# Converting float64 weights in the tile that keeps them, and two tiles instead of four in the head of a fused attention and MLP kernel

## The chip, the cores and the metric

The kernel runs on one core of one Trainium2 chip. The metric is the device time of one execution in microseconds (us). The engines are named as in the profile: PE (TensorE, with PEld for its weight loads), DVE (VectorE), ACT (ScalarE), POOL (GpSimd) and SP (SyncE), which issues nearly all DMA transfers. Each engine works off its own list of instructions strictly in order.

## The reference, cut to what matters

Three layers follow each other: an attention (a downsampled one plus a local band), a softplus MLP, and an expert layer that picks one expert for each token. Only the first two and the weights of the second bear on the change:

```python
x = attn_out.transpose(0, 2, 1, 3).reshape(B * S, H * D)   # 2304 tokens x 512
h = x @ w_in                                                # 512 x 2048
g = np.maximum(h, 0.0) + np.log1p(np.exp(-np.abs(h)))       # softplus
x = g @ w_out                                               # 2048 x 512
...                                                         # top-1 expert layer
```

`w_in` and `w_out` arrive as float64 (each is a float32 array times a float64 scalar). The engines work in float32, so the kernel has to convert both, 2 x 1 M values, on the chip.

## The kernel before

**Tiles of weights.** The hidden width of 2048 is cut into 16 chunks of 128. Chunk c has one tile of `w_in` (called i0 to i15 here, kept in `wi[:, c]`) and one of `w_out` (o0 to o15, kept in `wo[:, c]`), each 128 x 512. The list `conv` sets the order of conversion: i0, i1, o0, i2, o1, i3, o2, i4, o3 and so on to o15, 32 tiles.

**Conversion of one tile.** `load_raw` issues a DMA of 512 KB into one of six buffers named `raw`, in which every value is two 32-bit words. The same six buffers hold the raw q, k and v of the attention for batches 1 to 3 (`qr`, `kr`, `vr`), so loads of both kinds wait for each other's buffers. Then one instruction on ACT, `f64_top` (L617, called the *top* below), reads the upper words and writes 32 bits that hold the exponent and the high mantissa bits. Three instructions on DVE in `from_f64` finish the tile: a shift (L625), a merge of the sign (L628) and a merge of the low mantissa bits (L629). The last of them writes the tile of `wi` or `wo`; with it the raw buffer is free. Between the top and L629 the value lives in a tile `cva`, of which there are two, so that a top waits until the L629 of the tile before the last is done:

```python
t = mlp.tile([128, 512], I32, tag="cva", name="cva", bufs=2)
A.activation(t.bitcast(F32), raw[:, :, 1].bitcast(F32), AF.Abs, scale=F64_REBIAS)
```

**Head.** The first 18 steps (`HEAD`) run the attention of batch 0, software-pipelined in stages. `conv_to(n)` is called from step 4 on and converts up to tile n of the list; until the head ends its instructions are given priority over the rest (`ahead(-50)`). With the counts of this kernel the head converts four tiles: i0, i1, o0, i2.

**Block 0.** The MLP goes in six blocks of 384 tokens. Block 0 uses plain float32 matmuls (`xN` with `wi`, L768; for the first eight chunks `gN` with `wo`, L809). For chunk c the PE makes `ph`, ACT makes the softplus's Abs, Exp and Ln (L777, L778, L779), DVE adds the positive part and writes `gN` (L786), and the PE multiplies `gN` with `wo[:, c]` into `py`. The remaining tiles are converted during block 0, two for each chunk, and the attention of batch 1 runs between (its results `pS`, `pA`, `pO`). Blocks 1 to 5 and the expert layer need no more conversions.

**What sets the order.** The order on each engine isn't written out: a scheduler places the instructions by priority, program order and its own estimate of times when the program is built. A change in tiles or in the place of a call can therefore move neighbours as well.

Of the kernel before, what the change touches and what calls it, by code (L numbers as in the profile page):

```python
# [9 lines left out]
F32 = mybir.dt.float32  # L10
F32R = mybir.dt.float32r
I32 = mybir.dt.int32
U32 = mybir.dt.uint32
AF = mybir.ActivationFunctionType
ALU = mybir.AluOpType
# [26 lines left out]
F64_REBIAS = 2.0 ** -112  # L42
# [6 lines left out]
LAG = LAGS[-1]  # L49
HEAD = 12 + LAG  # L50
C0 = 3
CR = 1

NATIVE = 1


@with_exitstack
def band_attention__softplus_mlp__top1_moe(
# [15 lines left out]
    V, A, G, T = nc.vector, nc.scalar, nc.gpsimd, nc.tensor  # L74
# [28 lines left out]
    mlp = ctx.enter_context(tc.tile_pool(name="mlp", bufs=2))  # L103
    wi = wpool.tile([128, NC1, CC, 128], F32, name="wi")
    wo = wpool.tile([128, NC1, DM], F32, name="wo")
    ydram = drp.tile([NB, 128, CC, TB], F32, name="ydram")

    def ahead(n):

        return tc.high_priority(n) if n else nullcontext()  # L110
# [187 lines left out]
    class Local:  # L298
# [58 lines left out]
        def st_PV(self):  # L357
# [7 lines left out]
            if blk not in xT:  # L365
                if blk < NATIVE:
                    xT[blk] = xpool.tile([128, CC, TB], F32, tag="xT", name="xN")
                else:
                    xT[blk] = xpool.tile([128, 2, CC, TB], F32R, tag="xT", name="xT")
            if blk < NATIVE:  # L370
                xf = xT[blk][:, self.hp, off:off + TH].rearrange("p (g r) -> p g r", r=FACTOR)
            else:
# [5 lines left out]
                in1=odb.to_broadcast([128, TH // FACTOR, FACTOR]), op=ALU.add)  # L378
            if blk < NATIVE:
                return  # L380
# [201 lines left out]
    def attn_to(p):  # L582
        while pos[0] < p:
            _, n, st = pieces[pos[0]]
            pos[0] += 1
            run_piece(n, st)

    done = set(x[1:] for x in pieces)
    for n in range(NOLD):
        for st in range(6):  # L590
            if (n, st) not in done:
                late = n >= 14
                t = {3: 8.0, 4: 8.6 if late else 8.0, 5: 9.0 if late else 8.3}[st]
# [18 lines left out]
                    )  # L612


    def f64_top(raw):
        t = mlp.tile([128, 512], I32, tag="cva", name="cva", bufs=2)
        A.activation(t.bitcast(F32), raw[:, :, 1].bitcast(F32), AF.Abs, scale=F64_REBIAS)  # L617
        return t

    def from_f64(raw, t, dst):  # L620

        lo, hi = raw[:, :, 0], raw[:, :, 1]
        ins = V.tensor_scalar(t, t, 3, None, ALU.logical_shift_left)  # L625
        if started[0]:
            tc.keep_in_program_order(ins)
        V.scalar_tensor_tensor(t, hi, -0x80000000, t, ALU.bitwise_and, ALU.bitwise_or)  # L628
        V.scalar_tensor_tensor(dst.bitcast(I32), lo, 29, t, ALU.logical_shift_right, ALU.bitwise_or)  # L629

    conv = [("i", 0), ("i", 1), ("o", 0)]
    for c in range(1, NC1):
        conv += ([("i", c + 1)] if c + 1 < NC1 else []) + [("o", c)]
    cpos, lpos = [0], [0]
    raws, tops = {}, {}

    def load_raw(n):
        while lpos[0] < min(n, len(conv)):
            kind, c = conv[lpos[0]]
            raw = mlp.tile([128, 512, 2], I32, tag="raw", name="raw", bufs=RAWB)  # L640
            if kind == "i":
                nc.sync.dma_start(
                    out=raw.rearrange("p (c f) w -> p c (f w)", c=CC),
                    in_=w_in[:, c * 128:(c + 1) * 128].bitcast(I32).rearrange("(c p) f -> p c f", p=128))
            else:
                nc.sync.dma_start(out=raw.rearrange("p f w -> p (f w)"),
                                  in_=w_out[c * 128:(c + 1) * 128, :].bitcast(I32))
            raws[lpos[0]] = raw
            lpos[0] += 1

    def conv_to(n):
        while cpos[0] < min(n, len(conv)):
            i = cpos[0]
            load_raw(i + 2)
            kind, c = conv[i]
            with ahead(0 if started[0] else -50):
                for k in range(i, min(i + 2, lpos[0]) if started[0] else i + 1):
                    if k not in tops:
                        tops[k] = f64_top(raws[k])
                from_f64(raws.pop(i), tops.pop(i), wi[:, c].rearrange("p c f -> p (c f)") if kind == "i" else wo[:, c, :])  # L660
            cpos[0] += 1
            load_raw(i + 2)

# [9 lines left out]
    def split_wi(n, c):  # L673
        if n < NATIVE:
            return
        wis[n, c] = split(wi[:, c] if n < NB else mo["w1"][:, :, c * 128:(c + 1) * 128], "wis")

    def plain_g(n, c):

        return n < NATIVE and c < NC1 // 2  # L680

# [80 lines left out]
    def mlp_H(n, c):  # L762
        ps = psa.tile([128, 512], F32, tag="pa", name="ph")
        wt = None if n < NATIVE else wis.pop((n, c))
        i = 0
# [257 lines left out]
    for st in range(HEAD):  # L1023
        attn_to(pre_end[st])
        if st >= C0 - 5 + LAG:
            conv_to((st - C0 + 5 - LAG) * CR // 4 + 1)
        if st == 9 + LAG:
            split_wi(0, 0)
    started[0] = True
# [15 lines left out]
    for i, (n, c) in enumerate(seq[:NMLP]):  # L1045
# [20 lines left out]
        if n == 0:  # L1066
            conv_to(max(cpos[0], 3 + 2 * c + 1, CB + (33 - CB) * (2 * c + 1) // 32))
# [21 lines left out]
        if n == 0:  # L1089
            conv_to(max(cpos[0], 3 + 2 * c + 2, CB + (33 - CB) * (2 * c + 2) // 32))  # L1090
# [97 lines left out]
    p, q, pos_q = stages[-1]  # L1188
# [57 lines left out]
```

## Time and profile before

| | |
|---|---|
| time, median of 3 runs | 764.23 us (763.49 to 765.17) |
| time of the profiled execution | 765.59 us |
| its span, first to last instruction | 763.8 us |
| PE busy | 734.5 us, 96% of the span |
| DVE, ACT, POOL busy | 487.6, 462.3, 419.2 us |

The profiled execution took 1.8 us more than its span and 1.36 us more than the median. Times in the rows further down count from the start of the span. "Busy" means that an instruction is in the engine; for PE this includes matmuls that run slowly or overlap, so a busy PE isn't a PE at its peak.

### The profile page before, as it was taken

What the parts mean: (1) busy time and instruction counts of PE and PEld (TensorE: products, weight loads), DVE (VectorE), ACT (ScalarE), POOL (GpSimd) and SP (SyncE); (2) the same over time, 40 slices, a digit from 0 to 9 for tenths busy, and PEclk for the clock granted to TensorE, in tenths of its full rate; (3) what the DMA queues carried; (4) which work ended last, traced back from release to release, by engine and by line L of the source; (5) the groups of instructions that cost most, each with busy time, mean ns of one, the idle gap of its engine ahead of it and who ended that gap; (6) DMA issues with size and microseconds to landing.
All of it is one profiled execution on the core that took longest, in us unless ns stands there. A gap on an engine that the chain in (4) does not pass through costs nothing.

```text
span 763.8 us, 13608 instructions
## 1 busy us (share of the span) xinstructions
PE 734.5 (96%) x4917; PEld 655.8 (86%) x4918; DVE 487.6 (64%) x933; ACT 462.3 (61%) x1196; POOL 419.2 (55%) x381
## 2 busy tenths in 40 slices
PE   5989899999999999999999999999999999999995
PEld 5765567699999999998999999999997989899894
DVE  6999779765879555788645554346994484284222
ACT  5955565676667757666766665666864364365332
POOL 3553207376565655665565656666778465455542
PEclk9989999999999999999999999999999999999999
DMA  8987755115230511241001100530011022002002
GB/s 190 203 188 195 226 165 177 45 39 106 50 75 9 112 33 23 42 87 42 14 2 23 43 1 1 221 125 1 4 68 55 21 63 83 0 1 83 1 0 88
DMA packets 111446, 55.45 MB, mean 73 GB/s; under 512 B 89593, under 2 KB 102411, under 8 KB 111371
## 3 DMA queue, kind: packets, MB, share of 16 engines
q1 hardware_dynamic: 111083, 53.98, 26.8%
q8 instruction: 41, 0.67, 0.4%
q10 hardware_dynamic: 288, 0.52, 0.2%
q14 instruction: 34, 0.28, 0.1%
HBM read 45.05 MB, written 9.44 MB: 71 GB/s over the span
## 4 chain that ended last, share of the span: by engine, by line
PE 69%; DVE 16%; ACT 4%; issue 4%; DMA 3%; POOL 2%; SPq 1%; DVEq 0%; ACTq 0%; POOLq 0%
PE ph L771 19%; PE py L812 19%; PE py L1130 11%; PE ph L973 9%; PE pS L462 2%; DVE cva L628 2%; PE pO L495 2%; DVE cva L625 2%; PE pA L488 1%; PE py L809 1%; DVE xs L954 1%; DMA vr<-in_v_dram 1%; DVE wi L629 1%; DMA raw<-in_moe_w_in_dram 1%; PE ph L768 1%
## 5 line engine op out<-in xcount | busy, mean ns | idle before, releaser
L812 PE MATMUL py<-g,wos 128*128 128x384 f32 x1056 | 209.1, 341 | 2.6 <-DVE y L818 1.2
L812 PEld LDWEIGHTS py<-g,wos 128*128 128x128 f32 x1056 | 182.6, 188 | 9.2 <-issue 1.4
L771 PE MATMUL ph<-xT,wis 128*128 128x384 f32 x960 | 182.2, 337 | 0.0
L771 PEld LDWEIGHTS ph<-xT,wis 128*128 128x128 f32 x960 | 166.7, 188 | 1.1
L668 POOL TENSOR_TENSOR wis<-wi,wis 128x512 fp32r<-128x512 f32 x80 | 104.1, 1304 | 73.0 <-ACT wis L667 66.2
L668 POOL TENSOR_TENSOR wos<-wo,wos 128x512 fp32r<-128x512 f32 x88 | 118.2, 1344 | 45.0 <-ACT wos L667 44.7
L777 ACT ACTIVATE ga<-ph 128x384 f32<-128x384 f32 x96 | 46.6, 485 | 64.3 <-PE ph L771 61.3
L793 DVE SCALAR_TENSOR_TENSOR ph<-ph,ga 128x384 f32<-128x384 f32 x80 | 44.7, 560 | 58.9 <-ACT ga L779 58.6
L973 PE MATMUL ph<-xs,ws 128*128 128x384 f32 x378 | 73.9, 336 | 1.2 <-DVE u L978 1.2
L978 DVE TENSOR_TENSOR u<-ph,u 128x384 f32<-128x384 f32 x60 | 33.3, 555 | 60.2 <-PE ph L973 59.9
L973 PEld LDWEIGHTS ph<-xs,ws 128*128 128x128 f32 x378 | 67.1, 188 | 4.8 <-DVE u L978 1.6
L667 ACT CAST wos<-wo 128x512 fp32r<-128x512 f32 x88 | 54.4, 618 | 26.4 <-PE py L812 23.6
L1130 PE MATMUL py<-wos,gs 128*128 128x512 f32 x270 | 69.0, 394 | 0.7 <-POOL gs L984 0.4
L1130 PEld LDWEIGHTS py<-wos,gs 128*128 128x128 f32 x270 | 50.0, 188 | 9.8 <-POOL gs L984 0.8
L668 POOL TENSOR_TENSOR wos<-w2s,wos 128x512 fp32r<-128x512 f32 x24 | 33.5, 1395 | 34.7 <-ACT wos L667 34.7
L779 ACT ACTIVATE ga<-ga 128x384 f32<-128x384 f32 x96 | 50.3, 525 | 2.1
L778 ACT ACTIVATE ga<-ga 128x384 f32<-128x384 f32 x96 | 50.3, 525 | 0.3
L481 POOL TENSOR_TENSOR pls<-pls,plst 128x420 f32<-128x420 f32 x18 | 16.0, 891 | 61.2 <-DVE plst L480 54.4
L475 ACT ACTIVATE pls<-pls,plst 128x70 f32<-128x70 f32 x108 | 36.7, 341 | 21.4 <-DVE plst L473 21.3
L794 DVE CAST g<-ph 128x384 fp32r<-128x384 f32 x80 | 44.0, 550 | 7.8 <-PE py L812 4.3
L667 ACT CAST wis<-wi 128x512 fp32r<-128x512 f32 x80 | 48.9, 611 | 0.0
L768 PE MATMUL ph<-xN,wi 128*128 128x384 f32 x128 | 45.6, 503 | 0.9 <-DVE gN L786 0.9
(195 smaller groups left out, 1232.4 us busy)
## 6 DMA issues: line engine op xcount, KB each, us to landing
raw<-in_moe_w_in_dram SPq DMA_DIRECT2D x16, 512.0 KB
raw<-in_moe_w_out_dram SPq DMA_DIRECT2D x16, 512.0 KB
lv<-in_v_dram SPq DMA_DIRECT2D x72, 70.0 KB
vr<-in_v_dram SPq DMA_DIRECT2D x16, 288.0 KB
ydram<-y SPq DMA_DIRECT2D x12, 384.0 KB
yb<-ydram SPq DMA_DIRECT2D x12, 384.0 KB
out_dram<-ob SPq DMA_DIRECT2D x16, 256.0 KB
qr<-in_q_dram SPq DMA_DIRECT2D x48, 72.0 KB
```

What stands on the lines that cost most here:

```text
L667: A.copy(w[:, 0], src)
L668: G.tensor_tensor(out=w[:, 1], in0=src, in1=w[:, 0].bitcast(F32), op=ALU.subtract)
L768: T.matmul(ps[:, :TB], wi[:, c, cc, :], xT[n][:, cc, :], start=(cc == 0), stop=(cc == CC - 1))
L771: T.matmul(ps[:, :TB], wt[:, w, cc, :], xT[n][:, x, cc, :], start=(i == 0), stop=(i == 3 * CC - 1))
L777: A.activation(a, ps[:, :TB], AF.Abs)
L778: A.activation(a, a, AF.Exp, scale=-1.0)
L779: A.activation(a, a, AF.Ln, bias=1.0)
L793: V.scalar_tensor_tensor(o, ps[:, :TB], 0.0, a, ALU.max, ALU.add)
L794: (A.copy if n < NATIVE else V.tensor_copy)(g[:, 0, :], o)
L812: T.matmul(yps[n][dc][:, :TB], w[:, a, dsl], g[:, b, :], start=(c == 0 and i == 0), stop=(c == NC1 - 1 and i == 2))
L973: T.matmul(ps[:, :TB], ops[:, w, a, cc, :], xop[p, x][:, l, cc, :], start=i == 0, stop=i == 5)
L1130: T.matmul(yps[n][t], g[:, a, t * 128:(t + 1) * 128], w[:, b, :], start=first and c == q and i == 0, stop=last and c == q + NQ and i == 2)
```

## The change

The tile `cva` goes. The top writes its 32 bits straight into the place in `wi` or `wo` where the weights will stand, and the three DVE instructions work there in place. And the head's `conv_to` is capped at `HEADC = 2`: it converts i0 and i1; o0 and i2 are converted when block 0's first call of `conv_to` asks for them.

```diff
+HEADC = 2
...
-    def f64_top(raw):
-        t = mlp.tile([128, 512], I32, tag="cva", name="cva", bufs=2)
-        A.activation(t.bitcast(F32), raw[:, :, 1].bitcast(F32), AF.Abs, scale=F64_REBIAS)
-        return t
+    def f64_top(raw, dst):
+        A.activation(dst, raw[:, :, 1].bitcast(F32), AF.Abs, scale=F64_REBIAS)
...
-    def from_f64(raw, t, dst):
+    def from_f64(raw, dst):
...
-        lo, hi = raw[:, :, 0], raw[:, :, 1]
+        lo, hi, t = raw[:, :, 0], raw[:, :, 1], dst.bitcast(I32)
         ins = V.tensor_scalar(t, t, 3, None, ALU.logical_shift_left)
...
         V.scalar_tensor_tensor(t, hi, -0x80000000, t, ALU.bitwise_and, ALU.bitwise_or)
-        V.scalar_tensor_tensor(dst.bitcast(I32), lo, 29, t, ALU.logical_shift_right, ALU.bitwise_or)
+        V.scalar_tensor_tensor(t, lo, 29, t, ALU.logical_shift_right, ALU.bitwise_or)
...
+    def weights(i):
+        kind, c = conv[i]
+        return wi[:, c].rearrange("p c f -> p (c f)") if kind == "i" else wo[:, c, :]
...
-                    if k not in tops:
-                        tops[k] = f64_top(raws[k])
-                from_f64(raws.pop(i), tops.pop(i), wi[:, c].rearrange("p c f -> p (c f)") if kind == "i" else wo[:, c, :])
+                    if k not in topped:
+                        topped.add(k)
+                        f64_top(raws[k], weights(k))
+                from_f64(raws.pop(i), weights(i))
...
-            conv_to((st - C0 + 5 - LAG) * CR // 4 + 1)
+            conv_to(min((st - C0 + 5 - LAG) * CR // 4 + 1, HEADC))
```

The lines of the changed kernel shift by one up to L617, where the top keeps its number; its DVE instructions are L624, L627 and L628, the softplus L781 to L783, `gN` L790. The scheduler then places things anew. Three places matter below.

**DVE at the end of the head.** `xN` (L376, then L377) is the last piece of block 0's input; the transposes of `qr` and `kr` belong to batch 1. Before:

```order
L335 TENSOR_REDUCE lst<-ls 128x3
L180 STREAM_TRANSPOSE qkT<-qr 128x576
L333 SCALAR_TENSOR_TENSOR ls<-pS,mask 128x210
L355 COPY laT<-pA 70x384
L204 TENSOR_REDUCE dqs<-qkT 128x144
L376 TENSOR_TENSOR xN<-pO,od 128x192
```

and now, where the `wi` rows are the conversion of i2:

```order
L627 SCALAR_TENSOR_TENSOR wi<-raw,wi 128x512
L347 RECIPROCAL lst<-lst 128x3
L336 TENSOR_REDUCE lst<-ls 128x3
L334 SCALAR_TENSOR_TENSOR ls<-pS,mask 128x210
L356 COPY laT<-pA 70x384
L181 STREAM_TRANSPOSE qkT<-qr 128x576
L628 SCALAR_TENSOR_TENSOR wi<-raw,wi 128x512
L377 TENSOR_TENSOR xN<-pO,od 128x192
```

Three of the four instructions from the transpose to `xN` moved away (ahead of the transpose or behind `xN`), and the last step of i2 came in. The conversion of o0 stands some 15 rows earlier; before, o0 and i2 were converted in the middle of the head.

**ACT at the first softplus of block 0.** `ga_887` (now `ga_871`) is chunk 0's softplus, `xT` a cast for block 1. Before:

```order
L341 ACTIVATE ls_845,lst_847<-ls_845,lst_847 128x70 x3
L384 CAST xT_918<-xf_919 128x192
L777 ACTIVATE ga_887<-ph_882 128x384
L778 ACTIVATE ga_887<-ga_887 128x384
L384 CAST xT_918<-xf_930 128x192
L779 ACTIVATE ga_887<-ga_887 128x384
```

and now, with the tops of i4 (`raw_957`) and o3 (`raw_984`):

```order
L342 ACTIVATE ls_836,lst_838<-ls_836,lst_838 128x70 x3
L617 ACTIVATE wi_95<-raw_957 128x512
L385 CAST xT_912<-xf_913 128x192
L781 ACTIVATE ga_871<-ph_866 128x384
L617 ACTIVATE wo_96<-raw_984 128x512
L782 ACTIVATE ga_871<-ga_871 128x384
L385 CAST xT_912<-xf_924 128x192
L783 ACTIVATE ga_871<-ga_871 128x384
```

Two tops stand among the first softplus's instructions. The load of i4 takes the raw buffer that i2's L628 frees; before, it took the one that the transpose of `qr` frees.

**ACT at chunk 3's softplus.** Before (`raw_1101` is i6, `raw_1120` is o5):

```order
L416 ACTIVATE pde_1050,pdn_1049<-pS_1040,pmx_1048 96x144 x3
L617 ACTIVATE cva_1103<-raw_1101 128x512
L777 ACTIVATE ga_1076<-ph_1071 128x384
L778 ACTIVATE ga_1076<-ga_1076 128x384
L617 ACTIVATE cva_1122<-raw_1120 128x512
L779 ACTIVATE ga_1076<-ga_1076 128x384
```

and now (`raw_1108`, `raw_1120`, `raw_1135` and `raw_1147` are o5, i7, o6 and i8):

```order
L417 ACTIVATE pde_1040,pdn_1039<-pS_1030,pmx_1038 96x144 x3
L617 ACTIVATE wo_96<-raw_1108 128x512
L617 ACTIVATE wi_95<-raw_1120 128x512
L617 ACTIVATE wo_96<-raw_1135 128x512
L781 ACTIVATE ga_1066<-ph_1061 128x384
L782 ACTIVATE ga_1066<-ga_1066 128x384
L617 ACTIVATE wi_95<-raw_1147 128x512
L783 ACTIVATE ga_1066<-ga_1066 128x384
```

The tops run three tiles further ahead here than before, and one still stands between Exp and Ln. On DVE, the conversion of i6 and the first step of i8 stand ahead of chunk 3's `gN` (before, that of i6 alone).

## Rows read from the trace of the kernel before

**Rows 1.** The page: PE's busy time, and the chain that ended last by engine.

```profile
PE 734.5 (96%) x4917; PEld 655.8 (86%) x4918; DVE 487.6 (64%) x933; ACT 462.3 (61%) x1196; POOL 419.2 (55%) x381
...
PE 69%; DVE 16%; ACT 4%; issue 4%; DMA 3%; POOL 2%; SPq 1%; DVEq 0%; ACTq 0%; POOLq 0%
```

**Rows 2.** Windows by stage; columns as its first line says.

```profile
core 0: us, PE busy (x) PEld busy (x) DVE busy (x) ACT busy (x) POOL busy (x), PEclk, DMA share, GB/s
0.00:55.00 55.00, 42.95 (x434) 35.23 (x436) 45.23 (x105) 37.07 (x137) 26.30 (x54) 0.96 0.89 196
55.00:162.00 107.00, 102.00 (x566) 69.17 (x563) 86.14 (x149) 65.10 (x181) 38.14 (x37) 0.97 0.52 147
162.00:764.00 602.00, 589.52 (x3923) 551.42 (x3922) 356.19 (x682) 360.17 (x881) 354.76 (x291) 1.00 0.17 48
```

**Rows 3.** Waits: who waited for whom, us in total, times, longest.

```profile
ACT cva L617 <- DVE wi L629: 12.7, 8, 2.3
...
ACT cva L617 <- DVE wo L629: 11.0, 10, 2.3
```

**Rows 4.** DVE groups of 33.9 to 43.2 us: count, busy us, mean ns, idle before.

```profile
L628 DVE SCALAR_TENSOR_TENSOR cva<-raw,cva 128x512 int32<-128x512 int32 x2 | 2.5, 1270 | 0.0
L625 DVE TENSOR_SCALAR cva<-cva 128x512 int32<-128x512 int32 x2 | 0.8, 417 | 0.0
L629 DVE SCALAR_TENSOR_TENSOR wi<-raw,cva 128x512 int32<-128x512 int32 x1 | 0.7, 693 | 0.0
L629 DVE SCALAR_TENSOR_TENSOR wo<-raw,cva 128x512 int32<-128x512 int32 x1 | 0.7, 673 | 0.0
```

**Rows 5.** Conversion instructions by line: ns min/median/max, first and last start.

```profile
L625 DVE TENSOR_SCALAR cva<-cva x32: 376/416/2464, 28.7 to 154.6; 128x512 int32<-128x512 int32 x32
...
L628 DVE SCALAR_TENSOR_TENSOR cva<-raw,cva x32: 650/691/1652, 29.6 to 155.5; 128x512 int32<-128x512 int32 x32
```

**Rows 6.** Timeline, end of the head: start us, us, instruction, [idle before <- releaser].

```profile
50.41 0.68 ACT L617 ACTIVATE cva<-raw 128x512 f32<-128x512 f32 x1 [0.31 <-DMA raw<-in_moe_w_in_dram]
...
54.78 0.78 DVE L180 STREAM_TRANSPOSE qkT<-qr 128x576 f32<-128x576 f32 x1 [0.33 <-DMA qr<-in_q_dram]
...
55.69 0.39 SPq L642 DMA_DIRECT2D raw<-in_moe_w_in_dram  x1
...
56.87 0.34 DVE L376 TENSOR_TENSOR xN<-pO,od 128x192 f32<-128x192 f32 x1
...
60.48 0.49 ACT L777 ACTIVATE ga<-ph 128x384 f32<-128x384 f32 x1
```

**Rows 7.** Timeline around chunk 3's softplus, 82 to 88.5 us.

```profile
82.01 0.69 DVE L629 SCALAR_TENSOR_TENSOR wi<-raw,cva 128x512 int32<-128x512 int32 x1
...
82.77 0.37 SPq L642 DMA_DIRECT2D raw<-in_moe_w_in_dram  x1
...
85.97 0.69 DVE L629 SCALAR_TENSOR_TENSOR wi<-raw,cva 128x512 int32<-128x512 int32 x1
86.69 0.66 ACT L617 ACTIVATE cva<-raw 128x512 f32<-128x512 f32 x1 [2.34 <-DVE wi L629]
...
87.25 0.51 ACT L779 ACTIVATE ga<-ga 128x384 f32<-128x384 f32 x1
...
87.80 0.56 DVE L786 SCALAR_TENSOR_TENSOR gN<-ph,ga 128x384 f32<-128x384 f32 x1 [1.14 <-ACT ga L779]
...
88.41 0.58 PE L430 MATMUL pA<-ident,pde 96*72 96x96 f32 x3 [2.11 <-DVE gN L786]
```

**Rows 8.** Windows of half a microsecond behind the load issued at 82.77; columns of Rows 2.

```profile
85.50:86.00 0.50, 0.50 (x4) 0.22 (x3) 0.47 (x2) 0.00 (x0) 0.00 (x0) 1.00 0.42 148
86.00:86.50 0.50, 0.30 (x4) 0.09 (x2) 0.50 (x1) 0.00 (x0) 0.00 (x0) 1.00 0.00 0
```

**Rows 9.** PE alone in time: 8 matmuls of `py` twice, and a later wait.

```profile
75.57 2.74 PE L809 MATMUL py<-gN,wo 128*128 128x384 f32 x8
...
88.78 4.37 PE L809 MATMUL py<-gN,wo 128*128 128x384 f32 x8
...
140.44 2.20 PE L812 MATMUL py<-g,wos 128*128 128x384 f32 x11 [0.92 <-POOL g L795]
```

**Rows 10.** Windows with the granted clock; columns of Rows 2.

```profile
80.00:90.00 10.00, 7.89 (x27) 4.65 (x26) 8.27 (x14) 6.35 (x20) 1.77 (x2) 0.93 0.63 212
140.00:150.00 10.00, 9.15 (x76) 6.78 (x77) 9.59 (x15) 5.31 (x11) 3.64 (x4) 1.00 0.09 22
```

More of the change, by code (lines that the diff above doesn't have):

```diff
@@ L634, in band_attention__softplus_mlp__top1_moe @@
     cpos, lpos = [0], [0]
-    raws, tops = {}, {}
+    raws, topped = {}, set()
+    def weights(i):
+        kind, c = conv[i]
+        return wi[:, c].rearrange("p c f -> p (c f)") if kind == "i" else wo[:, c, :]
     def load_raw(n):
@@ L654, in conv_to @@
             load_raw(i + 2)
-            kind, c = conv[i]
             with ahead(0 if started[0] else -50):
                 for k in range(i, min(i + 2, lpos[0]) if started[0] else i + 1):
-                    if k not in tops:
-                        tops[k] = f64_top(raws[k])
-                from_f64(raws.pop(i), tops.pop(i), wi[:, c].rearrange("p c f -> p (c f)") if kind == "i" else wo[:, c, :])
+                    if k not in topped:
+                        topped.add(k)
+                        f64_top(raws[k], weights(k))
+                from_f64(raws.pop(i), weights(i))
             cpos[0] += 1
```

## The prediction

> **What bounds the kernel now.** The page comes first: PE is busy for 96% of the span, and 69% of the chain that ended last is PE's [rows 1]. The windows by stage say where another engine can matter. From 162 us on, behind block 0, PE is busy for 589.5 of 602 us at the full clock [rows 2]; no weights are converted there and no instruction that matters is moved, so I take that stretch as unchanged. What the change can touch lies in the first 162 us: the head up to 55, where PE is busy for 43 of 55 us, DVE for 45 and the DMA engines for 0.89 of the time, and block 0 up to 162, where PE is busy for 102 of 107 us [rows 2]. So block 0 can give back about 5 us of idle PE, and a little more where the clock was low; the head can give back what its slowest chain lets go.
>
> Next, the waits. A top waited 23.7 us in 18 cases for an L629 on DVE, which means for one of the two `cva` tiles [rows 3]. ACT works in order, so what stands behind such a top, often the Exp or Ln of a softplus, waits too. This is the wait that the change takes away by name. It costs something only where PE then waits for that softplus, and the timeline shows one large case, at chunk 3. There a top waits 2.34 us until the L629 of i6 is done, Ln starts at 87.25, `gN` at 87.80, and PE, whose next bank of PSUM this `gN` frees, stands for 2.11 us [rows 7]. Then 8 matmuls of `py` take 4.37 us, against 2.74 for the same 8 at 75.57 [rows 9], while the granted clock of that stretch is 0.93 on average [rows 10], a mixture of the 2.4 GHz level and the 1.2 GHz one. That one stop costs 2.1 us and, in slow matmuls, 4.37 - 2.74 = 1.6 us more.
>
> **The change part by part.**
>
> *The same work, elsewhere.* No instruction of a conversion is added or removed: 32 tops and 96 DVE instructions before and after. The third DVE instruction now writes where it reads; the second did so before, and both have the same median (L628 691 ns; the L629 rows show 693 and 673) [rows 4, 5]. In place costs nothing.
>
> *Two tiles fewer in the middle of the head.* The conversions of o0 and i2 took 0.8 + 2.5 + 0.7 + 0.7 = 4.7 us of DVE between 33.9 and 43.2 us, with no idle time before any of them [rows 4]. This is the most that the head can gain: -4.7 us. They come back near the end of the head at about 0.42 + 0.69 + 0.69 = 1.8 us a tile, by the medians. But the end of the head waits for DMA, not only for DVE: ACT's top at 50.41 stood until its raw tile had landed, and DVE's transpose at 54.78 until `qr` had [rows 6]. What lies ahead of these two can be early without moving them. What counts is the way from the transpose to the last `xN`. It takes 56.87 - 54.78 = 2.1 us now; in the new order only the transpose (0.78) and i2's last step (0.69) stand there, 1.5 us. I take -0.6. The other bound is a loss of 0.7: i2's step stands ahead of `xN` and nothing else moves.
>
> The rows show what a moved conversion can cost when POOL works beside it: the two L628 in the head took 1270 ns in the mean against a median of 691, and the worst L625 2464 against 416 [rows 4, 5]. The Trainium skill ("SBUF — State Buffer", section "SBUF: two separate sides") gives a reason: DVE and GpSimd share a pair of ports under an exclusive lock, so a DVE instruction with two operands in SBUF, or in a two-port mode, is blocked for the whole of the other's instruction, and the reverse. By that rule the moved instructions would pay for each POOL operation that they meet, and as an estimate from that page one such meeting ahead of `xN` would take back the whole 0.6; the sum below would end 0.6 us higher. I stay with the medians, since i2's last step stands right behind a transpose that waited for DMA.
>
> *The first softplus.* The load of i4 now waits for the buffer that i2's last step frees, and this step stands one instruction (0.69 us) behind the transpose that freed it before: it is issued at about 55.69 + 0.7 = 56.4 us. Its top stands ahead of the cast and the Abs that started at 60.48 [rows 6]. A lone load needs some 3.1 us: the one issued at 82.77 moved its last bytes between 85.5 and 86.0 [rows 7, 8]. With the DMA engines full, as they are in the head, it will need longer. If it lands at 59.5, the top (0.68) hides in ACT's wait for the matmuls, 0 us. If it takes 4.4 us (an estimate: 3.1 and half of the 2.7 us that 512 KB take at the head's 196 GB/s [rows 2]), it lands at 60.8 and Abs starts at 60.8 + 0.68 + 0.35 = 61.8, 1.3 us late. I take the middle, +0.6, so the head ends as a wash.
>
> *Chunk 3.* The top between Exp and Ln no longer waits for `cva`; it is i8's now, and waits for its raw tile. This load is the one at 82.77, behind the L629 at 82.01 (i5) [rows 7]; its last bytes arrive by 85.9 [rows 8]. So the top starts at 85.9 and not at 86.69. Two more tops (2 x 0.6 us) stand ahead of the Abs, but Abs and Exp still end before 85.9. Ln then starts at 86.5, `gN` at 87.0: -0.8 us, and PE's stop shrinks from 2.1 to 1.3 us. The bounds are 0 (the load lands 0.8 us later) and -2.1.
>
> *The clock behind it.* Unknown for a stop of 1.3 us, so bounds: 0 and -1.6 us. The stop of 2.11 was followed by slow matmuls; the one of 0.92 us at 140.44 left the granted clock at 1.00 [rows 9, 10]. 1.3 is nearer to 0.92, so I take the whole -1.6.
>
> *The rest of block 0.* Other tops that waited stand where PE had other work, and the new order puts more tops ahead of DVE (three in a row before chunk 3's Abs). They find a new thing to wait for: their raw tile, whose load starts when a buffer is freed. I take 0, with bounds of -1.0 and +1.5: a stop like the 0.92 us at 140.44 gone, or one or two such stops more.
>
> Sum: -0.6 + 0.6 - 0.8 - 1.6 = -2.4 us. The profiled execution took 765.59, so 763.2 for it; this execution was 1.36 us above the median, and against the median of 764.23 the forecast is **761.8 us**.
>
> **The rivals.**
>
> *The wait changes its name.* Every top that no longer waits for DVE waits for a load that starts when DVE frees a raw buffer, so ACT stands as long as before and PE too; or chunk 3's stop shrinks and the clock falls anyway. For it: six raw buffers shared with q, k and v, tops placed as early as the scheduler thinks the data is there, and 0.31 us of waiting for a raw tile already before [rows 6]. Against it: the 0.8 us that the load at 82.77 has in hand. Gain 0 to 0.8: about 764.0 us.
>
> *The head was DVE's.* If the waits for DMA at 50.41 and 54.78 move forward with the rest, since the loads of `qr` and `kr` are no longer behind a raw tile of 512 KB, the full 4.7 us of DVE comes through and not 0: 761.8 - 4.1 = 757.7 us. For it: DVE has no idle time before these instructions [rows 4]. Against it: the DMA engines are busy for 0.89 of the head [rows 2], and the bytes up to i3 stay the same.
>
> *Slower: the tops stand in front of the first softplus.* If i4's load lands at 60.8 and o3's, some 2.7 us behind it, at 63.5, then Abs is 1.3 us late, and the top of o3 between Abs and Exp holds the Ln. The `gN` of chunk 0 is about 1.1 us late, PE waits, and as DVE does conversions without a break there, the later chain to chunk 3 comes 1.1 us late as well: +1.1 twice and no gain, 766.4 us. It decides when i4's load needs more than about 3.7 us from its issue.
>
> *A stop at chunk 3 that stays* belongs to the first rival. That the change doesn't do what it says is ruled out: the new order has no `cva`, and o0 and i2 stand where the text says.
>
> **How the numbers follow.** The measurement of this kernel can tell 0.2%, which is 1.5 us, from no change. I give 0.40 to the forecast (its own range is 759.8 to 762.7, with the bounds of the rest), 0.36 to the wait that changes its name (762.7 to 765.7), 0.08 to the head that gains all of DVE's time, and 0.16 to the slower case. Faster by over 0.2% is 0.40 + 0.08 = 0.48, within 0.2% is 0.36, slower is 0.16. For eight in ten the range leaves out about half of the case at 757.7 and the worse part of the slower one: 759.0 to 765.9 us.
>
> **What would show it.** Right: ACT has no waits for L628 in the changed kernel, and instead some for DMA of raw tiles; the Ln of chunk 3 about 0.8 us earlier against the matmuls of chunk 3, PE's stop before it under 1.5 us, the following 8 matmuls of `py` at 2.7 us; the first matmul of block 0 within 1 us of 55.3; and the stretch behind block 0 as long as before. Wrong: the head ends 2 us or more earlier (then DVE, not DMA, held it); the stop at chunk 3 as long as before, or gone with the same total; ACT standing for several us in front of the first Abs of block 0; or a difference that arises behind block 0.

## The result and the profile after

The changed kernel takes **773.7 us** (median of 4 runs, 772.2 to 775.4), the kernel before 764.7 us: 1.0118 times as long, with a 95% interval of 1.0088 to 1.0148. The forecast was 761.8 us with a range of 759.0 to 765.9, so it is wrong in sign and the time lies outside the range. The profiled execution took 772.74 us with a span of 770.6 us, 6.8 us more than before.

The page shows PE about as busy as before and a chain that runs more over DMA (7% against 3%) and less over DVE (8% against 16%) [rows 1]:

```profile
PE 736.2 (96%) x4917; PEld 657.2 (85%) x4918; DVE 482.7 (63%) x933; ACT 461.6 (60%) x1196; POOL 421.1 (55%) x381
...
PE 76%; DVE 8%; DMA 7%; ACT 4%; POOL 2%; issue 2%; SPq 1%; DVEq 0%; POOLq 0%; ACTq 0%
```

To see where 6.8 us arise, I cut the span at two matmuls that both kernels have: the first `ph` of block 0 (55.33 us before, 58.22 after) and the first `ph` of block 1 (155.02 and 161.19). The windows of after between these cuts:

```profile
core 0: us, PE busy (x) PEld busy (x) DVE busy (x) ACT busy (x) POOL busy (x), PEclk, DMA share, GB/s
0.00:58.22 58.22, 43.05 (x435) 35.27 (x437) 42.28 (x105) 37.37 (x136) 25.22 (x54) 0.94 0.82 185
58.22:161.19 102.97, 96.57 (x522) 63.95 (x522) 81.80 (x144) 58.83 (x167) 38.14 (x35) 0.95 0.52 153
161.19:770.60 609.41, 596.58 (x3962) 557.96 (x3961) 358.62 (x687) 365.42 (x896) 357.76 (x293) 1.00 0.17 47
```

Before, the three stretches took 55.33, 99.69 and 608.78 us, with 43.28, 94.69 and 596.50 us of PE. So the head is 2.9 us longer, block 0 is 3.3 us longer, and the rest 0.6. Of these, 3.1 us are idle PE in the head, 1.4 us idle PE in block 0 and 1.9 us the same matmuls at a lower clock (0.95 against 0.97).

Matmuls that both kernels have divide block 0 further. PE's wait for chunk 0's `gN` ends at 65.24 us before and at 68.72 after, 3.5 us late. The 81st `ph` matmul of block 0 starts 4.0 us late (timeline of before, then of after):

```profile
119.21 2.75 PE L768 MATMUL ph<-xN,wi 128*128 128x384 f32 x8
...
123.25 2.75 PE L772 MATMUL ph<-xN,wi 128*128 128x384 f32 x8
```

And block 1 starts 6.2 us late. So 2.1 of block 0's 3.3 us are lost behind 120 us, more than at the first softplus (0.6) and at chunk 3.

The waits of the tops have changed their name, and grown from 23.7 us in 18 [rows 3] to 33.5 us in 21 (who waited for whom, us in total, times, longest):

```profile
ACT wi L617 <- DMA raw<-in_moe_w_in_dram: 20.3, 12, 3.2
...
ACT wo L617 <- DMA raw<-in_moe_w_out_dram: 13.2, 9, 2.6
```

**End of the head.** Timeline of after, 52 to 58 us:

```profile
52.17 0.67 ACT L617 ACTIVATE wo<-raw 128x512 f32<-128x512 f32 x1 [2.04 <-DMA raw<-in_moe_w_out_dram]
...
53.78 0.66 ACT L617 ACTIVATE wi<-raw 128x512 f32<-128x512 f32 x1 [0.94 <-DMA raw<-in_moe_w_in_dram]
...
54.99 0.35 ACT L342 ACTIVATE ls<-ls,lst 128x70 f32<-128x70 f32 x1
...
56.14 0.17 DVE L346 TENSOR_SCALAR lst<-lst 128x3 f32<-128x3 f32 x1 [2.40 <-ACT ls L342]
...
56.51 0.54 DVE L356 COPY laT<-pA 70x384 f32<-70x384 f32 x1
...
57.11 1.18 PE L361 MATMUL pO<-laT,lv 70*64 70x64 f32 x12 [2.75 <-DVE laT L356]
...
58.22 2.93 PE L772 MATMUL ph<-xN,wi 128*128 128x384 f32 x4
```

Two tops (of o1 and i3) stand for 2.04 and 0.94 us on ACT until their raw tiles have landed. Behind them stand the attention's Exp (`ls`), which began at 51.88 us before and begin at 54.99 now. DVE waits 2.40 us for them, its copy of `laT` behind it is late, and PE stands for 2.75 us. ACT had other work to do, and did not pass the top: DVE had finished `dqs`, at 50.53, and the instruction that makes `dbd` from it ran at 54.34, behind both tops. (Of "strictly in order" the argument needs only ACT and DVE.) Why the tiles are late is seen in SP's queue:

```profile
32.53 0.50 SPq L696 DMA_DIRECT2D bias_b<-n_moe_modality_bias_dram  x1
...
44.80 0.39 SPq L646 DMA_DIRECT2D raw<-in_moe_w_in_dram  x1
45.71 0.49 SPq L650 DMA_DIRECT2D raw<-in_moe_w_out_dram  x1
46.32 0.37 SPq L646 DMA_DIRECT2D raw<-in_moe_w_in_dram  x1
```

The load at 44.80 is i2's. Before, it was issued at 32.95, right behind `bias_b`. `conv_to` issues a tile's load when it converts the tile before it (o0 for i2), so the cap moved i2's load with o0's conversion, by 12 us. The loads of o1 and i3 stand behind it and went out 1.2 and 1.3 us later than before (44.55 and 45.03). The DMA engines, busy for 0.85 of the time between 30 and 40 us before, are busy for 0.69 there now.

**Chunk 3.** Timeline of after around its softplus:

```profile
87.07 0.68 ACT L617 ACTIVATE wo<-raw 128x512 f32<-128x512 f32 x1
...
87.63 0.70 ACT L617 ACTIVATE wi<-raw 128x512 f32<-128x512 f32 x1
...
88.38 0.67 ACT L617 ACTIVATE wo<-raw 128x512 f32<-128x512 f32 x1
88.96 0.47 ACT L781 ACTIVATE ga<-ph 128x384 f32<-128x384 f32 x1
...
90.59 0.66 ACT L617 ACTIVATE wi<-raw 128x512 f32<-128x512 f32 x1 [0.61 <-DMA raw<-in_moe_w_in_dram]
...
91.15 0.51 ACT L783 ACTIVATE ga<-ga 128x384 f32<-128x384 f32 x1
...
92.30 0.68 PE L431 MATMUL pA<-ident,pde 96*72 96x96 f32 x3 [2.24 <-DVE gN L790]
```

The top between Exp and Ln waits 0.61 us and not 2.34 [rows 7], as forecast. Three tops stand in a row ahead of Abs, which begins 5.6 us later than before while PE is 3.8 us late here (its matmuls ahead of the stop start at 85.89 and 89.65). But Exp had ended at 89.98, 0.61 us before the top could start, so it was the top's own raw tile that held Ln. Its load was issued at 86.91, 4.1 us later than before, and its top started 3.7 us after that, not 3.1 as forecast. Against PE the top starts 0.9 us after those matmuls (90.59 - 89.65), where the forecast had it start with them (85.9) and before it was 0.8 us (86.69). So nothing was won: the stop is 2.24 us (2.11 before), and the 8 matmuls of `py` behind it, 2.74 us long at the full clock [rows 9], take 4.26 (4.37 before):

```profile
92.78 4.26 PE L813 MATMUL py<-gN,wo 128*128 128x384 f32 x8
```

**Behind 125 us.** PE stops for 0.88 us at 127.05 for `g`, and for 1.39 and 0.84 us at 130.62 and 132.03 for `plaT`, a DVE copy; before, it stopped there for 0.69, 0.92 and 0.41 us. The granted clock of 130 to 140 us is 0.83, and was 1.00 before. The copy of `plaT` stood behind a conversion step with a median of 0.42 us that took 2.88 us while two POOL instructions ran (timeline of after):

```profile
126.96 1.62 POOL L424 TENSOR_TENSOR pde<-pde,pdn 96x864 f32<-96x864 f32 x1
127.22 2.88 DVE L624 TENSOR_SCALAR wo<-wo 128x512 int32<-128x512 int32 x1
128.55 1.27 POOL L672 TENSOR_TENSOR wos<-wo,wos 128x512 fp32r<-128x512 f32 x1
...
130.62 0.57 PE L496 MATMUL pO<-plaT,lv 70*64 70x64 f32 x12 [1.39 <-DVE plaT L490]
```

### The profile page after: what moved, and what is told of

Its sections match the earlier page's. It is cut to its first block, busy times and chain, and to the rows that moved or that the text cites. A ratio compares the mean times of both kernels' runs of the same rounds, so it can differ in the third digit from the quotient of the medians.

```text
span 770.6 us, 13582 instructions
## 1 busy us (share of the span) xinstructions
PE 736.2 (96%) x4917; PEld 657.2 (85%) x4918; DVE 482.7 (63%) x933; ACT 461.6 (60%) x1196; POOL 421.1 (55%) x381
## 4 chain that ended last, share of the span: by engine, by line
PE 76%; DVE 8%; DMA 7%; ACT 4%; POOL 2%; issue 2%; SPq 1%; DVEq 0%; POOLq 0%; ACTq 0%
PE py L816 23%; PE ph L775 21%; PE py L1134 11%; PE ph L977 9%; DMA raw<-in_moe_w_in_dram 3%; PE pS L463 2%; PE pO L496 2%; PE ph L772 2%; PE pA L489 1%; DMA qr<-in_q_dram 1%; DMA vr<-in_v_dram 1%; DMA out_dram<-ob 1%; PE pO L441 1%; PE pS L406 1%; POOL wos L672 1%
## 5 line engine op out<-in xcount | busy, mean ns | idle before, releaser
L781 ACT ACTIVATE ga<-ph 128x384 f32<-128x384 f32 x96 | 46.5, 484 | 63.1 <-PE ph L775 62.0
L672 POOL TENSOR_TENSOR wos<-w2s,wos 128x512 fp32r<-128x512 f32 x24 | 33.5, 1396 | 33.9 <-ACT wos L671 33.9
L783 ACT ACTIVATE ga<-ga 128x384 f32<-128x384 f32 x96 | 50.3, 525 | 2.0
```

What stands on the lines that cost most here:

```text
L672: G.tensor_tensor(out=w[:, 1], in0=src, in1=w[:, 0].bitcast(F32), op=ALU.subtract)
L781: A.activation(a, ps[:, :TB], AF.Abs)
L783: A.activation(a, a, AF.Ln, bias=1.0)
```

## The experiments

Theory at the start: the cap's late load makes the head late (+3.5 us at the first softplus), and the rest is lost in block 0. The rival: without `cva` nothing keeps the tops from running ahead, and ACT stands for raw tiles wherever that is. A second rival: any change here reshuffles the order, and this one had bad luck. All runs in one table; "DMA" is how long the tops waited for raw tiles, in us and times, in the profiled execution:

| kernel | median us | ratio to before (95%) | first ph, block 0 / block 1 | DMA |
|---|---|---|---|---|
| before | 764.7 | 1 | 55.33 / 155.02 | 0.3, 1 |
| after (both edits) | 773.7 | 1.0118 (1.0088 to 1.0148) | 58.22 / 161.19 | 33.5, 21 |
| e1 in place alone | 770.3 | 1.0055 (1.0033 to 1.0076) | 57.21 / 159.68 | 29.0, 20 |
| e2 cap alone | 766.8 | 1.0008 (0.9989 to 1.0028) | 53.97 / 157.65 | 1.8, 1 |
| e3 both, i2's load early | 773.2 | 1.0102 (1.0068 to 1.0137) | 54.98 / 161.71 | 28.7, 21 |
| e4 both, tops behind softplus | 774.9 | 1.0106 (1.0066 to 1.0146) | 54.98 / 165.65 | 4.4, 1 |
| e5 before, three `cva` | 765.3 | 0.9992 (0.9962 to 1.0022) | 57.85 / 154.99 | 9.6, 5 |
| e6 before, `cva` freed early | 764.1 | 0.9959 (0.9926 to 0.9992) | 56.53 / 153.42 | 5.9, 3 |
| e7 in place, seven raw | 770.7 | 1.0054 (1.0027 to 1.0081) | 56.99 / 161.22 | 23.7, 20 |
| e8 both, seven raw | 773.4 | 1.0101 (1.0030 to 1.0173) | 55.89 / 162.97 | 30.0, 22 |
| e9 in place, limit 2 | 764.0 | 0.9991 (0.9968 to 1.0013) | 56.01 / 151.01 | 0 |
| e10 both, limit 2 | 765.7 | 1.0009 (0.9995 to 1.0024) | 52.54 / 155.60 | 1.6, 1 |
| e11 as e6, and the cap | 768.3 | 1.0029 (1.0002 to 1.0055) | 57.01 / 157.14 | 7.4, 3 |
| e12 both, `plaT` on ACT | 772.1 | 1.0089 (1.0058 to 1.0119) | 57.66 / 160.16 | 32.8, 22 |
| e13 in place, limit 3 | 767.9 | 1.0029 (1.0011 to 1.0046) | 62.51 / 160.97 | 5.1, 3 |
| e14 in place, limit 4 | 769.3 | 1.0052 (1.0032 to 1.0072) | 58.62 / 157.96 | 12.3, 7 |
| e15 as e6, more rounds | 762.5 | 0.9971 (0.9949 to 0.9992) | 56.88 / 151.72 | 6.3, 3 |

Ratios compare runs on the same chip, and are what to go by. The cuts are those of one execution; that of e13 was 3.8 us above its median, that of e9 2.1 us below. A late first `ph` isn't yet a price: in e5 it comes 2.5 us late and block 1 on time, in e10 2.8 us early and block 1 0.6 us late. In all of them the stretch from block 1's first `ph` to the end takes 606.6 to 609.4 us (608.78 before), so hardly anything is lost behind block 0.

The diffs of e2, e5, e6 and e15 are against the kernel before, the others against the changed kernel.

**e1 and e2, the two edits apart.**

```diff
-HEADC = 2
+HEADC = 99
```

> In place without the cap (the head converts four tiles again). Theory, the late load: of the changed kernel's +6.8 us in the span, +3.5 belong to the cap, because it moves the load of i2 from 33 to 45 us and the DMA engines idle meanwhile; this kernel loads i2 early again, so the first ph comes at 55.3 us, as before, and the time is about 768 us (767 to 770), what is left being the loss at 125 to 134 us. Rival, tops without a limit: in place alone makes ACT stand for raw tiles, the head is late too and the time is about 773 us. Rival, the cap does all: 764.7 us.

```diff
-            conv_to((st - C0 + 5 - LAG) * CR // 4 + 1)
+            conv_to(min((st - C0 + 5 - LAG) * CR // 4 + 1, 2))
```

> The cap alone, with the two cva tiles kept. Theory, the late load: the head ends about 2.9 us later (first ph at 58.2) and the first softplus 3.5 us later, time about 768.2 us (767 to 770). Rival, tops without a limit: the cap costs nothing where a top still waits for cva, 764.7 us. Rival, order luck: the loss at 125 to 134 us shows up in neither kernel alone, and the two losses do not add up to that of both edits together.

The theory falls. In place alone costs 0.55%, 4.2 us, and its head is late although i2's load is early: there the tops of o1, i3 and i4 wait 1.57, 1.06 and 4.20 us. The cap alone costs nothing that can be told (0.6 us, interval of -0.8 to +2.1), though the span of its profiled execution, which was 1.4 us above the median, is 2.6 us longer. Together the two give 0.63% where both edits at once cost 1.18%, so the losses don't add up. That is what the rival of the order had foretold, and it stays open until e9 and e10. The cap's own mechanism is another: the loads bunch up at 44 to 49 us, those of `qr` and `kr` land late, and DVE stands for them with what PE needs queued behind (timeline of e2):

```profile
59.30 0.78 DVE L180 STREAM_TRANSPOSE qkT<-qr 128x576 f32<-128x576 f32 x1 [2.28 <-DMA qr<-in_q_dram]
...
61.23 0.52 PE L352 MATMUL pA<-ident,ls 128*70 128x128 f32 x3 [4.09 <-POOL ls L347]
...
63.52 0.78 DVE L180 STREAM_TRANSPOSE qkT<-kr 128x576 f32<-128x576 f32 x1 [2.08 <-DMA kr<-in_k_dram]
...
65.12 1.19 PE L360 MATMUL pO<-laT,lv 70*64 70x64 f32 x17 [3.37 <-issue]
```

**e3, the load back at its place.**

```diff
             conv_to(min((st - C0 + 5 - LAG) * CR // 4 + 1, HEADC))
+            load_raw((st - C0 + 5 - LAG) * CR // 4 + 2)
```

> The changed kernel, still converting only two tiles in the head, but the load of i2 stands at its old place (behind bias_b). Theory, the late load: the end of the head comes back by about 2.9 us (first ph at 55.5), time about 770 us. Rival, it is the conversions of o0 and i2 moved to the end of the head that make it late: nothing comes back, 773.7 us.

The head comes back (first `ph` at 54.98, chunk 0's `gN` 0.5 us earlier than before), so the late load did make the head late. But the time does not: 7.0 us are lost in block 0 in its place, with stops of 2.49 us at chunk 3 and 2.51 us for `plaT`. The late load is a part of the picture and not the price. The tops still wait for raw tiles 21 times, 28.7 us in all.

**e4, tops kept behind the softplus.**

```diff
-        A.activation(dst, raw[:, :, 1].bitcast(F32), AF.Abs, scale=F64_REBIAS)
+        ins = A.activation(dst, raw[:, :, 1].bitcast(F32), AF.Abs, scale=F64_REBIAS)
+        if started[0]:
+            tc.keep_in_program_order(ins)
...
-                for k in range(i, min(i + 2, lpos[0]) if started[0] else i + 1):
+                for k in range(i, i + 1):
```

> The changed kernel with the tops of block 0 kept in the order in which the program is written, so that they stand behind a softplus and never ahead of its Abs or between Abs and Ln. Rival, tops without a limit: if tops ahead of the softplus cost PE its waits in block 0, the stop at chunk 3 (2.2 us) and the 1 us at the first softplus go, about 769 us. Theory, the late load: the head stays late (first ph at 58.2), and the tops cost little beyond it: 772 to 774 us; tops placed this late can also make the conversions late for py, then above 775 us.

ACT's waits for raw tiles fall to 4.4 us, and the time does not. The edit changes more than it was meant to. Around 60 us DVE waits 3.02 and 2.96 us for `qr` and `kr`, and PE stops for 4.54 us at 64.61. The top of o0 now comes at 66.7 us (32.4 in the changed kernel), the conversions are late, and PE waits for them: 1.25 and 0.89 us for `wo` before `py` at 73 and 77 us. So this run says nothing on the rival, except that few waits for raw tiles don't make a kernel fast.

**e5 and e6, `cva` kept, but looser.**

```diff
-        t = mlp.tile([128, 512], I32, tag="cva", name="cva", bufs=2)
+        t = mlp.tile([128, 512], I32, tag="cva", name="cva", bufs=3)
...
```

> The kernel before with a third cva tile (the router's four small tiles share these buffers, to make room): a top may run one tile further ahead, nothing is written in place, the head converts four tiles. Theory, tops without a limit: with in place alone at +4.2 us and nothing else changed, a third tile gives part of that loss, 766 to 768 us, and ACT's waits at L617 turn from DVE to DMA in part. Rival, writing in place costs by itself: 764.7 us. Rival, order luck: anything between -2 and +5 us, and not in step with ACT's waits for DMA.

```diff
-        ins = V.tensor_scalar(t, t, 3, None, ALU.logical_shift_left)
+        d = dst.bitcast(I32)
+        ins = V.tensor_scalar(d, t, 3, None, ALU.logical_shift_left)
+        t = d
```

> Two cva tiles, no cap, but the first DVE step already writes into wi or wo and the other two work there in place, so cva is free two steps earlier. Theory, tops without a limit: a top still runs at most two tiles ahead, so most of the loss stays away, 764.5 to 767 us. Rival, writing in place costs by itself (two of three steps are in place): 767 to 769 us. Rival, order luck: anything between -2 and +5 us.

Neither loses, though e5's tops wait for raw tiles 5 times, 9.6 us in all, and e6, where two of the three DVE steps work in place, is faster than before. Working in place on DVE is not what costs. What e1 has beyond e6 is the top that writes straight into `wi` or `wo`, and with it no limit on how far the tops run.

**e7 and e8, more raw buffers.**

```diff
-RAWB = 6
+RAWB = 7
...
```

In both the output tile `ob` moves to the `raw` buffers too, and e7 is without the cap.

> In place without the cap, and the 4 KB of cva spent on a seventh raw buffer (the later output tile ob moves to raw as well). Theory, tops wait for raw tiles whose loads wait for a buffer: loads go out earlier, ACT's 29 us of waits for DMA at L617 shrink by a third or more, first matmul of block 1 at 157 us or earlier (in place alone 159.7), time 765 to 768 us. Rival, the DMA engines themselves set when a raw tile lands: as in place alone, 769 to 770 us.

> The changed kernel (in place and cap) with a seventh raw buffer. Theory, raw buffers: 33.5 us of waits for DMA at L617 shrink to 20 or so, first matmul of block 1 at 158 us (161.2 now), time 769 to 771 us. Rival, the DMA engines: 773.7 us as now.

No gain. In e7 the tops wait 23.7 us in all, just what they waited for DVE in the kernel before, and yet it is 0.54% slower. So it isn't the sum of the standing that costs but where it stands. The meeting of DVE with POOL behind 120 us, which the changed kernel has at 127 us, comes again in these two and in e3, with the same durations in all three (a step of 3.25 us beside POOL instructions of 1.65 and 1.28 us). Timeline of e8:

```profile
124.12 1.65 POOL L424 TENSOR_TENSOR pde<-pde,pdn 96x864 f32<-96x864 f32 x1 [2.07 <-DVE pdn L423]
...
124.31 3.25 DVE L627 SCALAR_TENSOR_TENSOR wi<-raw,wi 128x512 int32<-128x512 int32 x1
125.73 1.28 POOL L672 TENSOR_TENSOR wos<-wo,wos 128x512 fp32r<-128x512 f32 x1
...
129.60 0.91 PE L496 MATMUL pO<-plaT,lv 70*64 70x64 f32 x12 [2.75 <-DVE plaT L490]
```

A conversion step of 0.69 us by the median takes 3.25 us and ends 0.55 us after the second of two POOL instructions; the copy of `plaT` stands four instructions behind it on DVE, and PE stops for 2.75 us. The window behind it shows a granted clock of 0.52:

```profile
130.00:140.00 10.00, 8.76 (x67) 7.91 (x65) 7.25 (x11) 5.24 (x11) 5.05 (x4) 0.52 0.45 123
```

**e9 and e10, in place with the limit put back.** The top of tile k takes as its bias a column of zeros that DVE works out from the finished tile k-2; e9 is without the cap.

```diff
...
+    def f64_top(raw, dst, k):
+        A.activation(dst, raw[:, :, 1].bitcast(F32), AF.Abs, scale=F64_REBIAS, bias=zs[k - 2] if k >= 2 else 0.0)
...
+                zs[i] = const.tile([128, 1], F32, tag="zs", name="zs", bufs=8)
+                V.tensor_scalar(zs[i], weights(i).bitcast(F32)[:, 0:1], 0.0, None, ALU.mult)
```

> In place without the cap, with the limit of two tiles put back by another way: the top of tile k takes as its bias a column of zeros that DVE works out from the finished tile k-2 (32 small DVE instructions more). Theory, the limit: it was the cva limit that kept tops behind, so the time comes back to the kernel before, 763 to 766.5 us, and block 1's first matmul to 153 to 156 us (in place alone 159.7). Rival, a top that writes straight into wi or wo costs by itself: 768 to 771 us. Rival, order luck: neither, with a stop at a new place.

> The changed kernel (in place and cap) with the same limit of two tiles. Theory, the limit: most of the 9 us come back, what is left is the cap's own cost of 1 to 3 us as in the cap-alone kernel, 765.5 to 768 us. Rival, the cap's late load of i2 is the larger part in the changed kernel: 769 to 771 us. Rival, straight writes: 773 us.

This settles that the missing limit is what costs. With it, in place costs nothing that can be told (0.9991), and of the 1.18% of the changed kernel 0.09% is left, whose interval holds no change. Each kernel here has an order of its own, so luck of the order would have to hit one side only: the six kernels without a limit (the changed kernel, e1, e3, e7, e8, e12) lie at 1.0054 to 1.0118, those that keep a limit of two tiles (e2, e6 and e15, e9, e10, e11) at 0.9959 to 1.0029. (In e4 the program order holds the tops instead.) Which of the waits costs how much isn't shown by this. No top of e9 waits for a raw tile:

```profile
ACT wi L619 <- DVE zs L668: 6.5, 3, 3.5
ACT wo L619 <- DVE zs L668: 6.3, 4, 2.3
```

At the end of the head the tops of o1 and i3 stand behind a whole group of Exp and wait for nothing (timeline of e9), where e1, the same kernel without the limit, stood 1.57 and 1.06 us:

```profile
50.12 0.74 ACT L619 ACTIVATE wo<-raw,zs 128x512 f32<-128x512 f32 x1
50.90 0.77 ACT L619 ACTIVATE wi<-raw,zs 128x512 f32<-128x512 f32 x1
```

And at chunk 3 no top stands between Abs and Ln, `gN` comes behind a conversion step of DVE and not behind a late Ln, and the stop shrinks to 0.47 us, with a granted clock of 1.00 in the 10 us from 90 on:

```profile
83.37 0.47 ACT L785 ACTIVATE ga<-ph 128x384 f32<-128x384 f32 x1
...
84.43 0.52 ACT L787 ACTIVATE ga<-ga 128x384 f32<-128x384 f32 x1
...
86.23 0.55 DVE L794 SCALAR_TENSOR_TENSOR gN<-ph,ga 128x384 f32<-128x384 f32 x1
...
86.83 0.44 PE L431 MATMUL pA<-ident,pde 96*72 96x96 f32 x3 [0.47 <-DVE gN L794]
```

**e11, the cap on the better kernel.** The diffs of e6 and e2 together.

> The kernel that frees cva after the first DVE step, and the cap of two tiles on top. Theory: the cap costs 1 to 3 us wherever it is put, so 765 to 767 us against 764.1 without it. Rival, the cap's cost came from one bad order only (the 4.1 and 3.4 us stops at 61 and 65 us of the cap-alone kernel): 763 to 764.5 us.

It loses 0.7% against e6 (0.6% against e15, the same kernel timed again); its 768.3 us lie above what either side expected. With e2, e10 and the changed kernel, the cap has been added to four kernels: +0.08%, +0.18% (e10 to e9), +0.63% (after to e1) and +0.70%. The first two can't be told from nothing. It helped nowhere, and its price hangs on what stands around it.

**e12, `plaT` off DVE.**

```diff
-            V.tensor_copy(self.aT[:, a, :], ps[:KW, :384])
+            A.copy(self.aT[:, a, :], ps[:KW, :384])
```

> The changed kernel, with the copies of plaT on ACT and not on DVE, where they stood behind conversion steps that POOL's work had stretched. Theory, a second loss: PE's stops of 1.4 and 0.8 us ahead of pO at 130 to 132 us go, and the slow clock behind them; block 1's first matmul at 158 to 159 us (161.2), time 770 to 772 us. Rival, another wait takes their place (the ga of DVE L797 or ACT's own tops ahead of the copies): 773 to 775 us.

Between the two. The stops for `plaT` go, block 1 begins at 160.16 and not 161.19; but stops of 1.42 us for `ga` at 131.62 and 2.25 us for `g` at 136.46 take most of it. The two intervals overlap (1.0058 to 1.0119 and 1.0088 to 1.0148), so no gain is shown; by the medians that place is worth 1 or 2 us at most.

This trace also shows something on the clock. The stop at chunk 3 is longer than in the changed kernel, and yet the 8 matmuls of `py` behind it run at full speed (2.77 us, against 4.26), with a granted clock of 1.00 from 90 to 100 us (0.83 there in the changed kernel):

```profile
93.02 0.44 PE L431 MATMUL pA<-ident,pde 96*72 96x96 f32 x3 [2.62 <-DVE gN L790]
93.30 2.77 PE L813 MATMUL py<-gN,wo 128*128 128x384 f32 x8
```

**e13 to e15, the dose, and the faster kernel again.** The diff of e9 with `zs[k - 3]` and `zs[k - 4]`; e15 is e6.

> In place without the cap, limit of three tiles (the bias comes from tile k-3). Theory, the limit, as a dose: ACT's waits for DMA at L617 lie between those with two tiles (none) and those without a limit (29 us), time between 764.0 and 770.3, so 765 to 768 us. Rival, any limit does it (a third cva tile cost nothing): 763.5 to 765.5 us. Rival, order luck: no order in the dose.

> The same with a limit of four tiles. Theory, the dose: near the kernel without a limit, since the six raw buffers seldom hold more than four converted tops; ACT's waits for DMA over 15 us, 767 to 770 us. Rival, any limit does it: 763.5 to 765.5 us. Rival, order luck: no order in the dose.

> The kernel that frees cva after the first DVE step, timed with more rounds: it is the only one whose interval lay wholly under that of the kernel before. If the gain is real the ratio is 0.994 to 0.998 again; if not, 0.998 to 1.002.

The dose is in order: limits of 2, 3, 4 tiles and none give 0.9991, 1.0029, 1.0052 and 1.0055, with 0, 3, 7 and 20 tops that wait for a raw tile. Waits of e14:

```profile
ACT wo L619 <- DMA raw<-in_moe_w_out_dram: 7.6, 4, 3.6
...
ACT wi L619 <- DMA raw<-in_moe_w_in_dram: 4.7, 3, 4.0
```

Of these steps only that from 2 to 3 is clear of the noise; those from 3 to 4 and from 4 to none aren't. Nor is three tiles always a loss: e5, with three `cva` tiles, has 0.9992 (0.9962 to 1.0022), and e13, whose three waits for raw tiles all stand at the end of the head, 1.0029 (1.0011 to 1.0046). So the limit of two is shown to matter, and the dose beyond it is no more than in keeping with that. And e15 repeats e6: freeing `cva` after the first step makes the kernel before 0.3 to 0.4% faster, and both intervals lie under 1.

## Why the prediction was wrong

The step that failed is in the first part. It called the wait for `cva` "the wait that the change takes away by name", priced it as a cost that goes, and put what that wait held back at nothing. Term by term, from the shifts of PE's matmuls: the head -0.6 forecast and +2.9 measured, the first softplus +0.6 and +0.6, chunk 3's stop -0.8 and +0.1, the slow matmuls behind it -1.6 and -0.1, the rest of block 0 nothing and +2.7, behind block 0 nothing and +0.6; in all -2.4 and +6.8.

**What bounds it.** Right in the main: all but 0.6 of the 6.8 us arose ahead of block 1, and PE's stops there were what to look at.

**Same work, in place costs nothing.** Right: e6 and e9 work in place and lose nothing.

**The head, -0.6.** Wrong in sign: +2.9. The step said that "the end of the head waits for DMA, not only for DVE" and took the loads as they were. It overlooked that the load moves with the call: i2's was issued at 44.80 and not at 32.95, and the two behind it landed later too. DVE's relief did come (busy for 6.5 of the 10 us from 30 on, against 10.0) and bought nothing, as that step said. e3 shows that with the load at its place the head is on time in the changed kernel. In e1 the head is 1.9 us late although the load is early; there the tops of o1 and i3 wait 1.57 and 1.06 us ahead of Exp, but that they are the whole reason isn't shown.

**The first softplus, +0.6.** The mechanism was right, and so was the size at `gN`, which is what PE waits for: it was 3.5 us late (68.11 and 64.64), of which 2.9 had come with the head. That is partly luck. Abs came at 65.84 and not 60.48, 2.5 us late beyond the head and not at most 1.3. i4's load was issued at 60.46 and not, as forecast, at 56.4, since the transpose of `qr` and i2's last step came that much later; it took about the 4.4 us that the step put up as its bad case (its top began at 65.01). Before, DVE's own conversion steps (2.46 and 0.96 us) stood ahead of this `gN`, which hid the rest.

**Chunk 3, -0.8, and the clock, -1.6.** Half right. The top between Exp and Ln did wait less (0.61 us), and Exp did end before its raw tile had landed. What failed is when that tile lands: the step took 85.9, the last bytes, as the start of the top, and the top started 3.7 and not 3.1 us after the issue, which itself came 0.4 us later against PE. So the stop stayed (2.24 us), and the slow matmuls with it. The clock's term went by the length of the stop, and e12 shows that the length alone doesn't decide: behind 2.62 us the clock stayed at 1.00, behind 2.11 and 2.24 us it fell. What does decide stays open here. e9 has a stop of 0.47 us and a clock of 1.00, by another order than the one forecast.

**The rest of block 0, 0 with bounds of -1.0 and +1.5.** Measured 2.7 us, 2.1 of it behind 120 us. The step knew that tops would wait for raw tiles, and priced this by one or two stops. The deeper error is the one named above. The wait for `cva` was also a limit: it kept the tops within two tiles of DVE, and a top that may start only then found its raw tile there in all but one case. Without it 20 (e1) or 21 (after) of 32 tops meet a tile that hasn't landed, and what stands behind them on ACT comes late. That it is the limit is shown by e9 and e10. That the waits for raw tiles carry the whole loss isn't: e4 waits 4.4 us and is 1.06% slower, e5 waits 9.6 us and is not. That the scheduler puts tops early because its estimate of a load is too short is argued from the order, not shown.

**DVE beside POOL.** The prediction stayed with the medians. In sum that holds: conversion steps took 69.6 us after and 71.4 before, 13 of 96 over 1 us in both. Ahead of `xN`, where the prediction weighed one, no meeting came (i2's last step took 0.65 us). But single meetings cost much where a copy for PE stands behind them: 3.25 us for the step at 124.31 of e8, which ended 0.55 us after the second POOL instruction. The Trainium skill ("SBUF — State Buffer", section "SBUF: two separate sides") says that such a DVE instruction, with two inputs in SBUF, is blocked for the whole of a GpSimd instruction that holds the shared ports; these rows agree, and here one step was held through two POOL instructions in a row. In the changed kernel a step with one tensor input took 2.88 us in the same place.

**The rivals.** "The wait changes its name" was the right mechanism with the wrong price, 764.0: it assumed that a wait for DMA costs what the wait for DVE did. "The head was DVE's" fell: DVE was relieved and the head ended later. The slower rival named a right place (tops ahead of the first softplus, where i4's load needed 4.55 us and so more than its 3.7) and stopped at 766.4; it had no term for the head. (The lower end of the forecast's own range, 759.8, doesn't follow from the bounds it names for the rest of block 0: 761.8 - 1.0 is 760.8.)

What stays open is what each stop of block 0 is worth: each kernel without a limit loses at other places (chunk 0, chunk 3, `plaT`, `g`), and e12 shows that taking one away brings out the next.

## What to carry to other kernels

A small number of buffers between two engines is also a limit on how far the first one runs ahead, and on an engine that works in order that limit protects everything else it does: before taking such a buffer away, count who will wait for the load instead, and keep a limit in another form, or free the buffer earlier, which here gained 0.3 to 0.4%. When work is moved, look up what its call issues besides: here a load moved by 12 us with it. And a total of waiting says little: with 23.7 us of it e7 is 4 us slower than the kernel before with the same 23.7 us; what counts is what stands behind.

## What the runs showed of the hardware

The load of 512 KB issued at 82.77 before moved its last bytes some 3.1 us later [rows 7, 8]; in the changed kernel the top that waited for the one issued at 86.91 started 3.7 us after the issue, though the DMA engines moved 315 GB/s from 89 to 90 us and only 11 GB/s from 90 to 91: from the last bytes to the top it was about half a microsecond, as an estimate from these windows. Of three issued within 1.6 us there (44.80, 45.71, 46.32), the tops started 3.7, 6.5 and 7.5 us after their issue. A stop of PE of 0.47 us left the granted clock at 1.00 (e9); behind a stop of 2.75 us it was 0.52 over 10 us (e8), a mixture of the 1.2 and the 2.4 GHz level that is nearly all 1.2; and a stop of 2.62 us left it at 1.00 (e12). A DVE conversion step of 0.69 us by the median took 3.25 us beside two POOL instructions of 1.65 and 1.28 us (e3, e7, e8).
